# Doubled tail columns for the transposes, weights loaded by whole rows, and a newly searched TensorE order in a two-layer attention and feed-forward kernel

The kernel runs on **one core of one Trainium2 chip**. The metric is the device time of one execution in microseconds (us), as the median of some runs. The profile is one execution, and all profiled runs in this text were fast ones.

## The reference, cut to what matters

```python
def _A_ref(x, mem0, Wq, Wk, Wv, Wo, seg_len):        # x [1, 2048, 576], 32 heads of 128, bf16
    mem = mem0                                       # 8 rows
    for s in range(n_seg):                           # 64 segments of 32 tokens
        h = concat([mem, x[:, s*32:(s+1)*32]])       # 40 rows
        q, k, v = h @ Wq, h @ Wk, h @ Wv             # each 576 -> 32 x 128
        p = softmax(where(mask, q k^T * scale, -1e9))
        o = (p v) @ Wo
        mem = o[:, :8]                               # goes into the next segment
        outs.append(o[:, 8:])
    return concat(outs)
# _B_ref: silu(x @ w1) * (x @ w3) @ w2, 576 -> 4608 -> 576
x = x + _A_ref(_layernorm(x), ...);  x = x + _B_ref(_layernorm(x), ...)
x = x + _A_ref(_layernorm(x), ...);  x = x + _B_ref(_layernorm(x), ...)     # the same weights again
```

The memory makes the 64 segments of a layer a chain. The kernel fills the waits by running segment s of layer 0 beside segment s - 7 of layer 1, in 71 steps.

## The kernel before

Matrices have 576 = 4 x 128 + 64 rows. The fifth chunk has only 64 rows, and Q, K and V need it in both halves of the 128 partitions: half the tail matmuls read the upper rows of the array, half the lower ones. So a group of 128 normalized tokens (tile XN) is transposed on TensorE into one PSUM bank, and from there copied to the tile HT in pieces. The fifth transpose takes columns 448 to 576, of which only the last 64 are new:

```python
def ln_tr(self, xn, b):
    for c in range(5):
        c0 = min(c * P, D - P)                       # the last one overlaps: 448
        self.mm(self.lnps(b)[:, c, :], self.T.XN[:, xn.i, c0:c0 + P], self.T.ident[:], True, True, is_transpose=True)

def ht_write(self, li, g, j, b):                     # one segment j of the group's four
    for x0, co, m in X_AT[self.kind(t, li), role(t)]:     # one piece (layer 0) or two of 24 and 8 (layer 1)
        self.cp(n, H_[:, 0:4, co:co + m], ps[:, 0:4, x0:x0 + m])
        for r in (0, R64):                                # the tail, into both halves
            self.cp(n, H_[r:r + R64, 4, co:co + m], ps[R64:P, 4, x0:x0 + m])

def load_qk(self, u):                                # u = 0..7: 512 columns of Wq and of Wk
    for kind, wd in ((0, self.a.wq), (1, self.a.wk)):
        self.dma(self.T.W[:, 4*kind:4*kind+4, c0:c1], wd[0:4*P, c0:c1].rearrange("(c p) n -> p c n", p=P))
    ...                                              # and the tails, 64 rows x 512 columns each
# order of the pieces: four of Q and K, four of V, four of Q and K, four of Wo
```

The order of all TensorE blocks is fixed by three strings, FIRST + FOUR x 11 + LAST, one letter to a block. Q and q are the projection to Q and K and its tail, S the scores, T the transpose of the probabilities, P their product with V, O and o the output projection and its tail, V v X x the V projections, F f W the feed-forward, `a` and `b` the transposes of a normalized group of layer 0 and layer 1, `n` that for the feed-forward, `p` the transpose of a group of step outputs (tile YTS). A period below is one repeat of FOUR. A planner in the kernel walks this order with estimated durations, gives each copy to ScalarE (ACT) or VectorE (DVE), and picks buffers; so a changed string or a changed copy also changes who does which copy.

```python
FOUR = (
    "QQqqpQQqqVSSvQnQqqFTQqfPSVvTFQPqfOFWOTooSfPXxWFTFfPfOOWooQQqqWFQqfSFQqfQQqqVXxvSSWWTQPqQTFPqfOFfSoWWFTOfPFOTWofP"
    "WFOfooQQqqQFfqFWWQfqVVSSvvQQqqFTWQqPfSTWQFfqFSPfOWWFfoTOPoTWPOaOoobWQQqqpQQSqqQQqqVSSXxvQqTQqPXSTOPoxTOPonTOPoOo"
)
```

## Time and profile before

| | before |
|---|---|
| median time | 2843.19 us (3 runs, 2841.11 to 2845.37) |
| TensorE (PE) busy / VectorE / ScalarE | 97% / 73% / 40% |
| copies HT from a bank / XTB from a bank | 558 / 96 instructions |
| first stage, until the second step starts | 63.66 us |
| the eleven repeats of FOUR | 1820.1 us |

A view's line for a group of instructions reads: start, length, engine, line, operation, output<-input, shapes, count, and in brackets the idle time of that engine just before and what ended it. PE and PEld are TensorE's matmuls and weight loads. "issue" as a releaser means that the engine waited for nothing that the profile shows. The lines of before stand in the prediction.

### The profile page before, as it was taken

How to read it: one execution, taken by the hardware profiler on the slowest of the kernel's cores; microseconds unless marked ns; L12 is line 12 of the kernel's file. 1: busy time of each engine (PE TensorE's matmuls, PEld its weight loads, DVE VectorE, ACT ScalarE, POOL GpSimd, SP SyncE). 2: the span in 40 equal slices, each digit the busy share in tenths (PEclk: the TensorE clock that was granted, in tenths of full speed). 3: DMA queues.
4: the chain of work that ended last, by engine and by line, in shares of the span. 5: the costliest groups of instructions: out<-in, count | busy, mean ns of one | idle time of the engine just before them, and what ended most of it. 6: DMA issues, size and time to landing. Idle time of an engine off the chain costs nothing.

```text
span 2838.2 us, 136886 instructions
## 1 busy us (share of the span) xinstructions
PE 2741.1 (97%) x60909; PEld 2257.2 (80%) x60909; DVE 2069.6 (73%) x5743; ACT 1144.9 (40%) x3629; POOL 328.4 (12%) x399
## 2 busy tenths in 40 slices
PE   5999999999999999999999999999999999999998
PEld 3787878788887878888787888878788887878786
DVE  4677767777777677777767777776777777777775
ACT  1434443443434344343434434343443435343332
POOL 1111110110101011010101101010110101010110
PEclk8999999999999999999999999999999999999998
DMA  9072514234241433424243342414334242423468
GB/s 301 4 201 81 167 48 142 70 103 139 62 136 58 139 88 99 138 62 136 59 138 89 96 140 63 135 57 139 88 99 138 63 135 63 141 80 107 142 176 242
DMA packets 493425, 323.84 MB, mean 114 GB/s; under 512 B 26680, under 2 KB 488000, under 8 KB 492832
## 3 DMA queue, kind: packets, MB, share of 16 engines
q1 hardware_dynamic: 489808, 308.15, 37.4%
q8 instruction: 476, 7.80, 1.2%
q0 software_dynamic: 3024, 6.93, 0.8%
q14 instruction: 117, 0.96, 0.1%
HBM read 310.26 MB, written 2.36 MB: 110 GB/s over the span
## 4 chain that ended last, share of the span: by engine, by line
PE 92%; DVE 3%; ACT 2%; DMA 2%; issue 1%; SPq 0%; POOL 0%; DVEq 0%; ACTq 0%
PE bank L539 80%; PE YB L539 12%; ACT HT L542 1%; DVE HT L545 1%; DMA W<-in_A_Wk_dram 1%; SPq L548 0%; DMA WO<-in_A_Wo_dram 0%; DVE XN L545 0%; DVE XR L545 0%; ACT OT L542 0%; DVE HTT L545 0%; DVE PB L545 0%; DVE STAT L545 0%; DVE LNS L545 0%; DVE SME L545 0%
## 5 line engine op out<-in xcount | busy, mean ns | idle before, releaser
L539 PEld LDWEIGHTS <-W 128*128 128x128 bf16 (+1 forms) x29040 | 1228.7, 99 | 156.6 <-issue 57.4
L539 PE MATMUL bank<-HT,W 128*128 128x80 bf16 (+3 forms) x22720 | 821.3, 198 | 23.4 <-ACT HT L542 11.6
L539 PE MATMUL bank<-XTB,W 128*128 128x256 bf16 (+3 forms) x6320 | 659.3, 262 | 0.2 <-DVE HT L545 0.2
L893 POOL MEMSET PB<- 128x1024 bf16 x284 | 270.0, 951 | 2117.9 <-PE bank L539 1837.0
L542 ACT ACTIVATE QKT<-bank 128x64 bf16<-128x64 f32 (+1 forms) x1371 | 316.6, 317 | 353.1 <-PE bank L539 347.8
L539 PE MATMUL YB<-OT,WO 128*128 128x80 bf16 (+3 forms) x11360 | 434.9, 199 | 22.6 <-ACT HT L542 14.2
L539 PEld LDWEIGHTS <-WO 128*128 128x128 bf16 (+1 forms) x11400 | 390.7, 102 | 62.5 <-issue 45.8
L539 PE MATMUL bank<-WV,HT 128*32 128x512 bf16 (+1 forms) x6840 | 383.1, 384 | 7.8 <-DMA WV<-in_A_Wv_dram 7.7
L545 DVE CAST QKT<-bank 128x64 bf16<-128x64 f32 (+2 forms) x693 | 186.4, 316 | 189.5 <-PE bank L539 186.4
L539 PE MATMUL bank<-W2C,HTT 128*128 128x288 bf16 x2232 | 315.6, 289 | 0.0
L542 ACT ACTIVATE HTT<-bank 128x512 bf16<-128x512 f32 (+1 forms) x324 | 178.4, 552 | 292.5 <-PE bank L539 291.2
L545 DVE TENSOR_TENSOR PB<-SME,STAT 40x128 bf16<-40x128 f32 (+1 forms) x1004 | 283.6, 321 | 15.5 <-DVE STAT L545 0.5
L539 PEld LDWEIGHTS <-HT 128*32 128x32 bf16 (+1 forms) x6840 | 149.6, 95 | 173.3 <-issue 44.2
L545 DVE TENSOR_REDUCE STAT<-SME 104x8 f32<-104x320 f32 (+1 forms) x568 | 270.5, 476 | 17.2 <-ACT SME L542 11.7
L545 DVE SCALAR_TENSOR_TENSOR XR<-bank,XR 128x288 f32<-128x288 f32 x576 | 243.5, 449 | 29.2 <-PE bank L539 23.2
L539 PEld LDWEIGHTS <-HTT 128*128 128x128 bf16 x2304 | 211.8, 98 | 57.0 <-issue 4.1
L545 DVE SCALAR_TENSOR_TENSOR HTT<-HTT,bank 128x512 bf16<-128x512 bf16 (+1 forms) x324 | 201.1, 621 | 54.0 <-ACT HTT L542 51.9
L542 ACT ACTIVATE SME<-SME 104x320 f32<-104x320 f32 (+1 forms) x284 | 133.6, 471 | 234.5 <-DVE SME L545 233.2
L542 ACT ACTIVATE PTS<-bank 128x320 bf16<-128x320 f32 (+1 forms) x387 | 149.1, 415 | 189.0 <-PE bank L539 156.2
L545 DVE TENSOR_TENSOR HTT<-HTT,bank 128x512 bf16<-128x512 bf16 (+1 forms) x324 | 203.6, 628 | 23.9 <-PE bank L539 0.5
L542 ACT ACTIVATE V<-bank 128x512 bf16<-128x512 f32 x256 | 141.8, 596 | 179.8 <-PE bank L539 177.7
L545 DVE TENSOR_TENSOR SME<-bank,maskb 104x320 f32<-104x320 f32 (+1 forms) x284 | 134.1, 485 | 109.3 <-PE bank L539 87.3
(63 smaller groups left out, 1774.6 us busy)
## 6 DMA issues: line engine op xcount, KB each, us to landing
W<-in_B_w_dram SPq DMA_DIRECT2D x612, 256.0 KB, 3.6
W2C<-in_B_w_dram SPq DMA_DIRECT2D x306, 288.0 KB, 3.2
W<-in_B_w_dram SPq DMA_DIRECT2D x612, 32.0 KB, 3.1
W<-in_B_w_dram SPq DMA_DIRECT2D x10, 512.0 KB, 9.6
XR<-in_A_x_dram POOLq DMA_DIRECT2D x16, 288.0 KB, 3.6
WO<-in_A_Wo_dram SPq DMA_DIRECT2D x4, 1152.0 KB, 11.5
W<-in_A_Wq_dram SPq DMA_DIRECT2D x8, 512.0 KB, 7.3
W<-in_A_Wk_dram SPq DMA_DIRECT2D x8, 512.0 KB, 7.3
```

The costliest lines, as they stand in the source:

```text
L539: self.ch("PE", self.nc.tensor.matmul(out, lhsT=lhsT, rhs=rhs, start=start, stop=stop, skip_group_check=True, **k))
L542: self.ch("ACT", self.nc.scalar.activation(*a, **k))
L545: self.ch("DVE", getattr(self.nc.vector, fn_)(*a, **k))
L893: return lambda n: self.ch("POOL", self.nc.gpsimd.memset(self.T.PB[:, pb.i], 0.0))
```

## The change

The intent has three parts. **Copies**: XN gets 64 more columns, a copy of its last 64. The fifth transpose then delivers the tail in both halves of the partitions, so one copy moves all five chunks; two neighbouring segments go into one copy as well, and in the planner each copy of a group depends on the one before. **Load**: Wq, then Wk, then Wv, by whole rows of 8 KB, 128 rows to a transfer. **Order**: all three strings searched anew with this model. The work of TensorE stays. The planner's estimates changed too: no copy is counted under 0.19 us, a normalization as 0.12 to 0.18 us longer, a load at 380 GB/s in place of 340.

```diff
 def ln_norm(self, src, xn):
-    self.v("tensor_scalar", self.T.XN[:, xn.i, :], ...)
+    self.v("tensor_scalar", self.T.XN[:, xn.i, 0:D], ...)
+    self.v("tensor_copy", self.T.XN[:, xn.i, D:D + R64], self.T.XN[:, xn.i, D - R64:D])
 def ln_tr(self, xn, b):
-    c0 = min(c * P, D - P)
-    ... self.T.XN[:, xn.i, c0:c0 + P] ...
+    ... self.T.XN[:, xn.i, c * P:(c + 1) * P] ...
-def ht_write(self, li, g, j, b):
+def ht_write(self, li, g, js, b):                     # js: one segment, or two neighbours
-    for x0, co, m in X_AT[...]: (three copies: four chunks, tail, tail)
+    if k:   cp(56, 24, 0, 40, 24); cp(0, 152, 24, 8, 8)      # layer 1: two copies for two segments
+    else:   cp(X_AT[0, role(t)][0][1], 80, 0, 32, 32)        # layer 0: one copy
 def xtb_write(self, bi, b):
-    (three copies)
+    return lambda n: self.cp(n, self.T.XTB[:, :, bi * P:(bi + 1) * P], self.lnps(b))
 def ln_nodes(...):
-    node("AD", cost, wr(b), deps=[d] + more, ...)
+    node("AD", cost, wr(b), deps=[d] + more + out[-1:], ...)
-def load_qk(self, u): (512 columns of four chunks of Wq and Wk, and of the tails)
+def load_qk(self, kind):
+    for c in range(4):
+        self.dma(self.T.W[:, 4 * kind + c, :], wd[c * P:(c + 1) * P, :])
+    self.dma(self.T.W[kind * R64:(kind + 1) * R64, 8, :], wd[4 * P:D, :])
   (Wv the same way; FIRST and LAST all new)
 FOUR = (
+    "QQpqqQQqqVSSvnQQqqFTQqPfSVvQTFfqPOOSooTWFfPWFTOPfFOfooQQqqQQSqqVXxvWTQWFfqFQqPfSSWFWQfqXxFTWQqfPOTOooSWFfPFTOfPW"
+    "OooWFQfqQFfqWQFfqWQFfqVSSVvvQQqqWTWQPqSQTFfqFfPSWOWFTfoOPoTWPOOooabWQQqqpQQSqqQQqqVSSvXxTQqQqPTSXPxOToOPoTOPnOoo"
```

More of the change, by code (lines that the diff above doesn't have):

```diff
@@ L164, in actc @@
 def actc(*ns):
-    return sum(0.067 + n * 0.000833 for n in ns)
+    return sum(max(0.067 + n * 0.000833, 0.19) for n in ns)
 def dve(*ns):
-    return sum(0.065 + n / 960.0 for n in ns)
+    return sum(max(0.065 + n / 960.0, 0.19) for n in ns)
 def dveh(*ns):
-    return sum(0.065 + n / 1920.0 for n in ns)
+    return sum(max(0.065 + n / 1920.0, 0.19) for n in ns)
 def ew(*ns):
@@ L187 @@
 FIRST = (
-    "amQQVqqQSQvQqqTVSvqQQXqPSTPQxqTOoqSOoPOTPOooQQqqQSQqqQSVqvTQqPQqSQqTSPOOTooPaTOPOooQQqqQQSqqQSQqqVvQTQPqqSTVPSOO"
-    "TovXPoTxPOOooQQqqQQSqqQqSVQqTvSQqPQqTSPOToPOOTooPOoQQqqQSpQqqVVvvnQTFfqQqSFfPQOQqqSTFfPoSWXOTFPfoxTOoPWOoFQfqQqF"
-    "QQqSqfQFfqSVvTWQFqPfaFfTOSoPQQqqFSWTOFPfoTOPfoOWoVFvQqfFQfqWSVvQFfqFTQfqWPSQQqqQSFqfTQqPWFfSOTFfoPOWToPOoOboQQqq"
-    "QSqXxQQqqQSqTQSQqqVvXPSTOPoTxOoPTPOOooQQpqqQQSqqQQnqqVvSSQTFqfVvFPfQTOqPWFToSfFOfPXxOFTWofPFOoofQQqqQSXxqQWFfqVv"
-    "QQTqqSFPfSFQQqfqOFSofTWPFTOfPoFTOPfWOFooQqfFQqfQWQSqVqvQFqfSTWQqFPfSVvQTaQqqWFSFfPfOToPWTOoPObOXooxQQpqqQQSqQqqV"
@@ L193 @@
-    "QqSTSvQPQqqOTPSnXxTOoPoTOPOooVvpQQqqQqSQQqqnQSqVvTFfPQTOFPqfSQFqfXxOWTWoSoXxFfPFTOPfoWWOFfoFQqQfqQWQqqFWSSfVvQFf"
-    "qWQqFTQqfPSQWOTFqPfoSOWWTFfPoFTOPfWOooVvWQQqqFQfSqFWQqfQQSqqWTFfPQFSqQqfOTWWaFSPfVTOovWPTOoPobOoQQqqpQQSqqXVvxSQ"
-    "qQTqQqSQPqnTOPSXxoTOPoWTOPoOo"
+    "amQQqqQSqQqQSqQTQqqQSqSVvVvPXTPTOoOPoTOPoOoxQQqqQQSqqQSqVvQqQTSQPqqOTSoPTPOOToPaOooQQqqQQSqqQQSqVqvTQSqQPqVSTOPv"
+    "oTOoPXTOPOxooQQqqQSQqqQSqQqVSvQqTQqPTSOPToPOOTooPOoVvpQQqqQSQqqnVSvFfTQQqqQFPqfSFQfqXSTFfPOTOoWPxoTOFfPFOooWQqQq"
@@ new lines @@
+    "fFfSQQqqWQSQqqVvTFfPSFTfPQOQFfqqOTSWFooPfFTOPoaOoWfQQqqFQfqSVvWQFfqQqVSvWQqFfTQqFPfSTQqOWFofSPTFfPOWTOoPObooQQqq"
+    "XxSQQqqQQqqSTQVqvQqSPSTXxOPoTOPToPOOooQQqqpQQqqSVvnQQqqSTFfPFQqfSOTQqPFWOFffSVoTvXPxWOTFofPFOofoQQqqQqSQWQqqVvTQ"
+    "PSFfqQFqfSXxWTQFqPfOToSFafPOFofOTWPFOfooQFqfWQqVvSQqQFfqFQfqSQTWqQqPSFQqfVSvTWOPFFffoTOPoTWPOoOboQQqqQQSqqXVvxSQ"
+    "TpQqqXPxSQqTQqPOSoTOPoOTPnOooQQqqQpQSqQqqQnqVSvQTFfqFSPfVvQFfqTOFPfXxoSWWOTFfPXFTxofPOWOWooQQqqQqSQWFqfQQqqSTWFF"
+    "ffVvSQPqWTFQOqPfoSWTOFfPoFTOPfWOWooQFfqQqWFWQqfSVvFQqWfSFQqfQqWTQQPSqqVFTSvfPOWWoTFfOPoTWPOOooabQQqqpQQSqQqqVXxv"
@@ L196 @@
+    "STQQqqQPqSTOSoPXxOTWPTnoPOOoo"
 )
 FOUR = (
-    "QQqqpQQqqVSSvQnQqqFTQqfPSVvTFQPqfOFWOTooSfPXxWFTFfPfOOWooQQqqWFQqfSFQqfQQqqVXxvSSWWTQPqQTFPqfOFfSoWWFTOfPFOTWofP"
-    "WFOfooQQqqQFfqFWWQfqVVSSvvQQqqFTWQqPfSTWQFfqFSPfOWWFfoTOPoTWPOaOoobWQQqqpQQSqqQQqqVSSXxvQqTQqPXSTOPoxTOPonTOPoOo"
+    "QQpqqQQqqVSSvnQQqqFTQqPfSVvQTFfqPOOSooTWFfPWFTOPfFOfooQQqqQQSqqVXxvWTQWFfqFQqPfSSWFWQfqXxFTWQqfPOTOooSWFfPFTOfPW"
+    "OooWFQfqQFfqWQFfqWQFfqVSSVvvQQqqWTWQPqSQTFfqFfPSWOWFTfoOPoTWPOOooabWQQqqpQQSqqQQqqVSSvXxTQqQqPTSXPxOToOPoTOPnOoo"
@@ L200 @@
 )
 LAST = (
-    "QQpqQqqQSqnQQFqSqfVVSvvQTFPqfTOQqPWTOSoXxPoFTFfPfOOWQooFqfFQqWWQqfVXxvSWFQfqWFTSfQqQqPQFQSqqfOTFWPfSoWOTFoPfFWWT"
-    "OfPFOfooWQQqqFWQQqqSfVvQWFfqQSqTWQSqPFQfqVSvOWWTFfPFofTOPoTWPOoOobQQqqpQQSqqQQSqqVTSXxXvxQPqTQqPSWOToOoPTnPOOooQ"
-    "QqqQpQqqSVSvQqVvQnqTQPqSFfTQFqPfOoSOTFfPFTOofPXWOxooWQQqqVvFQfqWQSqWQFqfSFfTQqQWSqWFfPQFfqTOWWFPSofTOFfPWWOTFoof"
-    "PFOoWQqfQqWFQQqSqfFQfqVSvWQqTWQqSPQFqfFfSTWOWoFPfVvTWWPOoTOPbOooQqpQQqqXxSQnQqqQFfqSFfVvSTQPqFfTQqWSFOPfoFTOPfoT"
-    "OPWOFooQqfFQfqQQqqSVvQqSWTQqPQSVvqFTQPfqOOSooTFfPXxOTFPWOoofQQqqFfQQSqqWQQqqSFTfVFfvWSQqPQFfqOTSoFPfWTOoPFTOfPFO"
@@ L207 @@
-    "fooQQqqWQqVSVvvQqQQSTqQqQPqSqTOSPOoToPTPOOoopFfnWFfFFffFfWFWFffFfFWfFFffWFFffWFWfFfFFffWFfFfWW"
+    "QQqqVvpQQSqqQnQSqqQqTFPQfqVvSFOTFPfoSfTOPXxWFfOWTFofPFOooWWQfqQqFQfqSWQqXVvxSQWQqqFTfQFPfqSTOWWQPqFoSfFTOfPoWTOP"
+    "WOooFQqfQFfqQVSvqWQWFfqFSQfqQqWTWFSfPQQqqWFfSTWOFfPoVvTWPOoTOPobOoQQqqQQSqqQQpqqVSvSQqQTqXxSPTXxPOToOPoTWPOOoonQ"
+    "QqqpQqSVvQnQqqQSqTFfPVSvQQqqFTOPoSfOTFWWofPFTOfPXOWooQxqWQFqfVvSQQqFfqQQSqqQqTFfPSWWFQfqFfOWWFTSofPFTOWPfoTFPfOO"
+    "WooQQqqFQQqfqSWFWQFqffSVvWTWQQqqQqVSSvFPfFTOWWfFPfToOPoTWOPoOWboQQqqpQqSVXnvxQFfqQQqqTSSQPqFfQFfqWTSOPFTOofPFTof"
@@ L208 @@
+    "POOooWQFqfQFfqQQSqqVSvWQQqqTQPqSFQqfVTFfPvSOTOXooxPWTFPOOfooQQqqQFSqfVQFqfvWQTFSqQfqQFqPSfQqWTOPoSFfTOoPFWTOfPFO"
+    "fooQQqqQQSqqVvQWQSqqVvSQTQqPqTOPSoTFPOoOTofPOopnWFfFFfFffWFWfFfFfFfWFfWFfFFffWFfWFfFFffWFfFfWW"
 )
@@ L216, with make_nodes @@
     ustep, mode_pen, hor, wait, bulk, ff_split, last_win, tail_at = 0.0315, 0.1194, 0.0162, 0.141, 0.02, False, 2.5, -1.5
-def make_nodes(em, nseg, pools, o=Opt, dma_bw=230e3, load_bw=340e3):
+def make_nodes(em, nseg, pools, o=Opt, dma_bw=230e3, load_bw=380e3):
     ngrp = nseg // 4
@@ L246, in make_nodes @@
     ld_m0 = load("m0", kb(8, D), -10, em.load_m0())
-    ld_qk, ld_v, ld_o = {}, {}, {}
-    pr = -9.0
-    for what, i in [("qk", 0), ("qk", 1), ("qk", 2), ("qk", 3), ("v", 0), ("v", 1), ("v", 2), ("v", 3), ("qk", 4),
-                    ("qk", 5), ("qk", 6), ("qk", 7), ("o", 0), ("o", 1), ("o", 2), ("o", 3)]:
-        pr += 0.1
-        if what == "qk":
-            ld_qk[i] = load("ldqk", kb(1152, 512), pr, em.load_qk(i))
-        elif what == "v":
-            ld_v[i] = load("ldv", kb(576, 1024), pr, em.load_v(i))
-        else:
-            ld_o[i] = load("ldo", kb(1024, 576), pr, em.load_o(i))
+    ld_qk = [load("ldqk", kb(576, 4096), kd - 9.0, em.load_qk(kd)) for kd in (0, 1)]
+    ld_v = [load("ldv", kb(576, 4096), -7.0, em.load_v())]
+    ld_o = [load("ldo", kb(1024, 576), g - 6.0, em.load_o(g)) for g in range(NG)]
     b = banks(1)
@@ L273, in ln_nodes, with ht_set @@
         p_ = node("POOL", 0.45, em.ln_pow(xn), deps=[a], prio=prio, name=tag + "pow")
-        c = node("DVE", 0.34 if src is xn else 0.48, em.ln_norm(src, xn), deps=[p_], prio=prio, name=tag + "norm")
+        c = node("DVE", 0.46 if src is xn else 0.66, em.ln_norm(src, xn), deps=[p_], prio=prio, name=tag + "norm")
         b = Slot("bank", users=len(writes))
         d = node("PE", 5 * 0.056, em.ln_tr(xn, b), deps=[c], prio=prio, mode="full", acq=[b], rel=[xn], name=tag + "tr")
-        return [node("AD", cost, wr(b), deps=[d] + more, prio=prio, rel=[b], name=tag + "wr") for wr, cost, more in writes]
+        out = []
+        for wr, cost, more in writes:
+            out.append(node("AD", cost, wr(b), deps=[d] + more + out[-1:], prio=prio, rel=[b], name=tag + "wr"))
+        return out
     def ht_writes(li, g):
-        out = []
+        out, at = [], {}
+        for j in range(4):
+            at.setdefault((4 * g + j - role(4 * g + j + LAG * li)), []).append(j)
+        for te, js in at.items():
+            te += LAG * li - R_HT
+            cost = ewh(240, 80) if li and both(te + R_HT) else ewh(160 * len(js))
+            out.append(((lambda js: lambda b: em.ht_write(li, g, js, b))(js), cost, reads_ht.get(te, []) + reads_ht.get(te + 1, [])))
+        return out
+    def ht_set(li, g, nodes_):
+        i = -1
         for j in range(4):
             t = 4 * g + j + LAG * li
-            te = t - role(t) - R_HT
-            cost = ewh(96, 32, 24, 8, 24, 8) if li and both(t) else ewh(128, 32, 32)
-            out.append(((lambda j: lambda b: em.ht_write(li, g, j, b))(j), cost, reads_ht.get(te, []) + reads_ht.get(te + 1, [])))
-        return out
-    def ht_set(li, g, nodes_):
-        for j in range(4):
-            ht_ready[li, 4 * g + j + LAG * li] = nodes_[j]
+            i += j == 0 or role(t) == 0
+            ht_ready[li, t] = nodes_[i]
     vx_slots, vx_nodes, vx_pe, last_v = {}, {}, [None], [None]
@@ L327, in step @@
             sl, ev, last_v[0] = v_nodes("VM", t, pv_, o.vmt, (lambda k: lambda b, tail: em.vm(t, k, b, tail))(k), 2 if e else 4,
-                                     hm[:1] + hx + (list(ld_v.values()) if t == 0 else []), hm[1:])
+                                     hm[:1] + hx + (ld_v if t == 0 else []), hm[1:])
             for kk in ((k,) if e else (0, 1)):
@@ L342, in step @@
                 pq = t + o.qk + o.ustep * u
-                m_ = node("PE", 32 * mm80, em.qk(t, u, b), deps=hx + hm[:1] + ([ld_qk[u]] if t == 0 else []),
+                m_ = node("PE", 32 * mm80, em.qk(t, u, b), deps=hx + hm[:1] + (ld_qk if t == 0 else []),
                           prio=pq, mode="full", acq=[q] + b, name="QK")
@@ L423, in job @@
         prev_ff = last_up[0]
-        cost = ewh(512, 128, 128)
+        cost = ewh(640)
         for (bi, g) in reversed(ents):
@@ L588, in load_m0 @@
         return lambda n: self.dma(self.T.M0[0:MEM, :], self.a.mem0[0])
-    def load_qk(self, u):
+    def load_qk(self, kind):
         def f(n):
-            c0, c1 = u * 512, (u + 1) * 512
-            for kind, wd in ((0, self.a.wq), (1, self.a.wk)):
-                self.dma(self.T.W[:, 4 * kind:4 * kind + 4, c0:c1], wd[0:4 * P, c0:c1].rearrange("(c p) n -> p c n", p=P))
-            for kind, wd in ((0, self.a.wq), (1, self.a.wk)):
-                self.dma(self.T.W[kind * R64:(kind + 1) * R64, 8, c0:c1], wd[4 * P:D, c0:c1])
+            wd = (self.a.wq, self.a.wk)[kind]
+            for c in range(4):
+                self.dma(self.T.W[:, 4 * kind + c, :], wd[c * P:(c + 1) * P, :])
+            self.dma(self.T.W[kind * R64:(kind + 1) * R64, 8, :], wd[4 * P:D, :])
         return f
@@ L602, in wv, with load_v @@
         return self.T.WV[:, 0:4 * H * E].rearrange("p (c n) -> p c n", c=4)
-    def load_v(self, g):
+    def load_v(self):
         def f(n):
-            k, r = g // 2, g % 2
-            c0, c1 = g * 1024, (g + 1) * 1024
-            self.dma(self.wv(False)[:, :, c0:c1], self.a.wv[0:4 * P, c0:c1].rearrange("(c p) n -> p c n", p=P))
-            self.dma(self.wv(True)[r * R64:(r + 1) * R64, k * 1024:(k + 1) * 1024], self.a.wv[4 * P:D, c0:c1])
+            for c in range(4):
+                self.dma(self.wv(False)[:, c, :], self.a.wv[c * P:(c + 1) * P, :])
+            t = self.a.wv[4 * P:D, :].rearrange("p (k r n) -> p k r n", k=2, r=2)
+            for r in (0, 1):
+                self.dma(self.wv(True)[r * R64:(r + 1) * R64, :].rearrange("p (k n) -> p k n", k=2), t[:, :, r, :])
         return f
@@ L616, in load_xn @@
     def load_xn(self, g, xn):
-        return lambda n: self.dma(self.T.XN[:, xn.i, :], self.a.x[g * P:(g + 1) * P, :])
+        return lambda n: self.dma(self.T.XN[:, xn.i, 0:D], self.a.x[g * P:(g + 1) * P, :])
     def load_x(self, g, xr):
@@ L687, in src_ap @@
     def src_ap(self, src):
-        return self.T.XN[:, src.i, :] if src.pool == "xn" else self.T.XR[:, src.i, :]
+        return self.T.XN[:, src.i, 0:D] if src.pool == "xn" else self.T.XR[:, src.i, :]
     def ln_stats(self, src, xn):
@@ L708, in f @@
             L = self.T.LNS[:, xn.i]
-            self.v("tensor_scalar", self.T.XN[:, xn.i, :], self.src_ap(src), L[:, 12:13], L[:, 15:16],
+            self.v("tensor_scalar", self.T.XN[:, xn.i, 0:D], self.src_ap(src), L[:, 12:13], L[:, 15:16],
                    op0=ALU.subtract, op1=ALU.mult)
+            self.v("tensor_copy", self.T.XN[:, xn.i, D:D + R64], self.T.XN[:, xn.i, D - R64:D])
         return f
@@ L719, in f, with cp @@
             for c in range(5):
-                c0 = min(c * P, D - P)
-                self.mm(self.lnps(b)[:, c, :], self.T.XN[:, xn.i, c0:c0 + P], self.T.ident[:], True, True, is_transpose=True)
+                self.mm(self.lnps(b)[:, c, :], self.T.XN[:, xn.i, c * P:(c + 1) * P], self.T.ident[:], True, True, is_transpose=True)
         return f
-    def ht_write(self, li, g, j, b):
+    def ht_write(self, li, g, js, b):
         def f(n):
             ps = self.lnps(b)
-            t = 4 * g + j + LAG * li
-            H_ = self.ht(t)
-            for x0, co, m in X_AT[self.kind(t, li), role(t)]:
-                x0 += j * SEG
-                self.cp(n, H_[:, 0:4, co:co + m], ps[:, 0:4, x0:x0 + m])
-                for r in (0, R64):
-                    self.cp(n, H_[r:r + R64, 4, co:co + m], ps[R64:P, 4, x0:x0 + m])
+            t = 4 * g + js[0] + LAG * li
+            H_, x0, k = self.ht(t), js[0] * SEG, self.kind(t, li)
+            def cp(co, gap, src, apart, m):
+                d, r = H_[:, :, co:co + m], ps[:, :, x0 + src:x0 + src + m]
+                if len(js) == 2:
+                    d, r = (bass.AP(v.tensor, v.offset, [list(x) for x in v.ap][:-1] + [[by, 2], [1, m]]) for v, by in ((d, gap), (r, apart)))
+                self.cp(n, d, r)
+            if k:
+                assert len(js) == 2
+                cp(56, 24, 0, 40, 24)
+                cp(0, 152, 24, 8, 8)
+            else:
+                cp(X_AT[0, role(t)][0][1], 80, 0, 32, 32)
         return f
     def xtb_write(self, bi, b):
-        def f(n):
-            ps = self.lnps(b)
-            dst = self.T.XTB[:, :, bi * P:(bi + 1) * P]
-            self.cp(n, dst[:, 0:4, :], ps[:, 0:4, :])
-            for r in (0, R64):
-                self.cp(n, dst[r:r + R64, 4, :], ps[R64:P, 4, :])
-        return f
+        return lambda n: self.cp(n, self.T.XTB[:, :, bi * P:(bi + 1) * P], self.lnps(b))
     def v_mm(self, t, b, strips, tail):
@@ L1076, in fin_cast @@
     def fin_cast(self, xr, xn):
-        return lambda n: self.act(self.T.XN[:, xn.i, :], self.T.XR[:, xr.i, :], ACT.Copy)
+        return lambda n: self.act(self.T.XN[:, xn.i, 0:D], self.T.XR[:, xr.i, :], ACT.Copy)
     def store(self, g, xn, last):
-        return lambda n: (self.dma if last else self.swdma)(self.a.out[g * P:(g + 1) * P, :], self.T.XN[:, xn.i, :])
+        return lambda n: (self.dma if last else self.swdma)(self.a.out[g * P:(g + 1) * P, :], self.T.XN[:, xn.i, 0:D])
 class Tiles:
@@ L1137 @@
     T.XTB = sp.tile([P, 5, 2 * P], BF, name="XTB")
-    T.XN = sp.tile([P, pools["xn"], D], BF, name="XN")
+    T.XN = sp.tile([P, pools["xn"], D + R64], BF, name="XN")
     T.LNS = sp.tile([P, pools["xn"], 16], F32, name="LNS")
```

## The prediction

> **What bounds the kernel now.** I read the page first, then the table by stages, then TensorE's waits and the instruction timeline around them.
>
> ```profile
> span 2838.2 us, 136886 instructions
> ...
> PE 2741.1 (97%) x60909; PEld 2257.2 (80%) x60909; DVE 2069.6 (73%) x5743; ACT 1144.9 (40%) x3629; POOL 328.4 (12%) x399
> ...
> PE bank L539 80%; PE YB L539 12%; ACT HT L542 1%; DVE HT L545 1%; DMA W<-in_A_Wk_dram 1%; SPq L548 0%; DMA WO<-in_A_Wo_dram 0%; DVE XN L545 0%; DVE XR L545 0%; ACT OT L542 0%; DVE HTT L545 0%; DVE PB L545 0%; DVE STAT L545 0%; DVE LNS L545 0%; DVE SME L545 0%
> ```
>
> TensorE is busy 97% of the span and is 92% of the chain that ended last. The change keeps all 60,909 matmuls, so only TensorE's idle time (97.1 us = 2838.2 - 2741.1), its slow-clock time and its changes of array shape can move. The table by stages (first column the stretch, then length, busy us by engine, granted clock, DMA share, GB/s) says where the idle time is:
>
> ```profile
> 0.00:63.66 63.66, 30.70 (x706) 21.69 (x707) 26.65 (x69) 10.76 (x34) 10.99 (x27) 0.89 1.05 324
> 63.66:532.60 468.94, 454.97 (x11278) 376.03 (x11277) 341.51 (x983) 194.04 (x645) 59.99 (x69) 0.99 0.38 109
> 532.60:2356.00 1823.40, 1792.29 (x38490) 1479.61 (x38486) 1355.03 (x3751) 762.05 (x2394) 204.52 (x243) 1.00 0.36 103
> 2356.00:2801.20 445.20, 430.38 (x9999) 353.25 (x9998) 324.27 (x886) 169.21 (x534) 52.32 (x60) 0.98 0.44 128
> ```
>
> 33.0 us are idle before the second step starts at 63.66 us, with the DMA share over 1: the first step waits for weights. Another 14.0, 31.1 and 14.8 us lie in the three later stages. The third is eleven equal periods of 165.8 us (four steps each, the string FOUR). One period's waits, in the timeline (start, length, engine, instruction, count, idle before it and who ended it; cut to the place that matters):
>
> ```profile
> 1195.86 0.69 ACT L542 ACTIVATE HT<-bank 128x128 bf16<-128x128 bf16 x3 [0.77 <-PE bank L539]
> 1196.58 0.61 DVE L545 COPY HT<-bank 128x128 bf16<-128x128 bf16 x3 [1.02 <-ACT HT L542]
> 1197.22 0.69 ACT L542 ACTIVATE HT<-bank 128x128 bf16<-128x128 bf16 x3 [0.67 <-DVE HT L545]
> 1197.93 0.22 ACT L542 ACTIVATE HT<-YB 128x64 bf16<-128x64 f32 x1
> 1197.94 0.61 DVE L545 COPY HT<-bank 128x128 bf16<-128x128 bf16 x3 [0.75 <-ACT HT L542]
> 1198.20 0.34 PE L539 MATMUL YB<-OT,WO 128*64 128x80 bf16 x8 [0.97 <-ACT HT L542]
> ...
> 1198.58 0.58 DVE L545 TENSOR_SCALAR XN<-XR,LNS 128x576 bf16<-128x576 f32 x1
> ...
> 1199.22 0.45 PE L539 MATMUL bank<-ident,XN 128*128 128x128 bf16 x5 [0.68 <-DVE XN L545]
> ```
>
> One transposed group is copied to HT by twelve instructions that ACT and DVE run strictly in turn, 1195.86 to 1198.55: 2.69 us. The copy of the new memory (HT<-YB) queues behind them on ACT, the normalization (XN) behind them on DVE, and TensorE waits 0.97 + 0.68 us. In every second period the throttle then halves the clock for one interval:
>
> ```profile
> 1199.80:1203.20 3.40, 3.40 (x38) 2.87 (x37) 2.07 (x12) 1.51 (x8) 0.00 (x0) 0.50 0.33 95
> 1203.20:1206.60 3.40, 3.40 (x98) 3.27 (x96) 2.93 (x11) 2.74 (x11) 0.59 (x1) 1.00 0.24 84
> ```
>
> [...] (1) [...] The trace shows the half clock for 3.4 us at 1199.8, but after a stretch only partly idle (2.36 of 4.00 us busy just before)[...]. (2) [...] on DVE 128x128 into HT takes 224 ns, 128x32 174; on ACT 278 and 197. A quarter of the elements costs over 70% of the time. (3) [...] 326 GB/s while Wq and Wk come in pieces of 512 and 64 KB, 379 while Wo comes in pieces of 1152 KB:
>
> ```profile
> DMA packets 5602, 6.20 MB, mean 326 GB/s; under 512 B 288, under 2 KB 4860, under 8 KB 5602
> ...
> DMA packets 4076, 4.55 MB, mean 379 GB/s; under 512 B 72, under 2 KB 4073, under 8 KB 4073
> ```
>
> (the DMA view of 3 to 22 us and of 48 to 60 us).
>
> **The change part by part.**
>
> *Loading.* Wq, Wk and Wv are 3 x 4.72 = 14.16 MB. At 326 to 330 GB/s they take 43.2 us; in DMAs of 1 MB at Wo's 379 they would take 37.4. Sixteen transfers (with the tails of 64 rows) replace forty. I take that as 5.8 us sooner: Wq complete at about 16 us, Wk 28, Wv 41, the last Wo piece at 55 to 56 instead of the 61.5 where the chain now leaves it ("DMA WO" 49.34 + 12.16). The price: no projection can start before Wk is complete, where now it starts at 15.1 us. So TensorE has the whole first step after 28 us. From rows of the timeline: eight Q and K blocks of 32 matmuls near 0.9 us plus tails, scores, transposes and slow clock, some 13 us, end near 41 as Wv arrives. After that come two V blocks at 2.3 (4.6), one further V block (2.4), four output blocks with tails at 1.3 (5.2), three transposes and four PV blocks (2.8), changes of shape and evacuation waits (2 to 3): 17 to 18 us. So the second step starts at 58 to 60 against 63.66. Gain 4 to 6 us; I take **5**.
>
> *Copies.* A first-layer group goes from 12 instructions to 3 (160, 320, 160 elements), a second-layer one from 24 to 4 (240 and 80 twice), XTB from 3 to 1. By the slopes of (2), 0.84 ns per element on ACT and 0.52 on DVE: 305 + 440 + 241 = 0.99 us in place of 2.69, and (372 + 237) + (282 + 199) = 1.09 in place of the 4.80 from 1199.70 to 1204.50. XTB 640 elements: 0.70 on ACT for 1.14, 0.49 on DVE for 0.88. Against it one copy of 64 columns per normalization, near 0.16 us x 64 = 10 us of DVE, each on the way to the transpose. Busy time falls from 141 us (HT 59.0 + 49.1, XTB 22.7 + 10.5) to about 63 with the new copies. DVE at 73% and ACT at 40% bound nothing, so almost none of these 78 us is gain in itself; what counts is TensorE's wait.
>
> *Order.* In the built kernel the period's end reads O, O, tails, then the first-layer transpose, then the second-layer one. On ACT the memory copy now stands ahead of the HT copies, and on DVE so does the normalization. From the starts of matmuls (they count pipelined time better than the idle column): that tail started 1.16 us late, and elsewhere, where no HT copy is in the way, the same wait is 0.51, so 0.65 is gained; the second-layer transpose's lateness of 0.77 goes; the half clock costs about 1.6 us (38 matmuls where 98 fit, but many of them 288 wide), in every second period, so 0.8. Against it: the strings' changes between ways of using the array (full, half rows, strips of columns) go from 109 to 112 per period and from 2,115 to 2,150 in all; one costs 95 ns (an 80-column matmul is followed after 36 ns by its like and after some 131 by another shape), so 0.28 per period, 3.3 us in all. Net 0.65 + 0.77 + 0.8 - 0.28 = 1.94 per period, x 11 = **21 us**.
>
> In the stage before, the same chain stands at 84.96 (1.18 idle), 222 to 228, 368.81 (1.70) and a half-clock interval at 370: about **6 us**. In the stage after, TensorE waits 1.8 us for HT at 2679 and the clock halves at 2681: **3 us**.
>
> Sum: 2843.2 - 5 - 21 - 6 - 3 = **2808 us**, 1.2% less.
>
> **Rivals.** *The gap is only filled otherwise*: the new order has other tight places, and the 64-column copy and the chained copies lengthen the way from XN to the next step. The old order too was searched, and lost 3 us per period to what its search had not seen. Against it: the chained copies are what the hardware did anyway (each group waits for the one before), so this search sees them. It would leave loading and a little: 2830 to 2840. *The load does not speed up*: rows of 1 KB and of Wv's 2 KB run alike (326 and 330 GB/s), so longer rows may give nothing; then the late start of TensorE costs and the first step ends at 63 to 66: 2813 to 2816. *The search closes nearly all gaps*: waits of 0.44 and 0.34 in the period, and a 0.7 wait for YTS in every second one, would go too, with more in the stages before and after: 50 to 60 us in all, 2785 to 2793. For over 2% the kernel must fall below 2786, that is recover 57 of 97 idle us, and part of those is the load, which cannot vanish.
>
> **Range and chances.** The load is sure to 4 us, the period to 1 us (11 us in all), the two other stages to 5. Added in one direction this is 20 us: 2787 to 2829. Faster by over 2%: 0.10; within 2%: 0.89; slower: 0.01.
>
> **What would show it.** In the changed profile: GB/s of the first 50 us near 375, not 325; the second step's first matmul at 58 to 60 us; HT from bank in about 109 instructions and XTB in 32; a chain of about 1.0 and 1.1 us in place of 2.69 and 4.80; a period of 163 to 164.5 us; no half-clock interval in most periods. A period still at 165.8 with a wait on another tile, or GB/s unchanged, would prove me wrong.

"The slopes of (2)" come from the four measured copies there: (278 - 197) / 96 = 0.84 ns per element on ACT, (224 - 174) / 96 = 0.52 on DVE. The 0.16 us for an added copy was an estimate; the nearest copy in the trace of before, HT<-mem0T with 128x40, took 164 ns.

## The result

The changed kernel took **2800.55 us** (median of 4 fast runs, 2798.39 to 2805.53), the kernel before 2844.28 us beside it. The ratio is **0.985** (95% interval 0.9832 to 0.9867), 1.5% less: within 2%, and inside the range of 2787 to 2829, 7.5 us under the predicted 2808. A ratio here is the mean time of one kernel's fast runs over that of the other's fast runs of the same rounds, so not quite the ratio of the medians. The results of all kernels were correct. The medians of the kernel before beside the experiments were 2846.88 (e1 to e4), 2846.20 (e5, e6, e8, e9) and 2844.97 us (e7, e10).

The page of the changed kernel:

```profile
span 2798.6 us, 136339 instructions
...
PE 2730.5 (98%) x60909; PEld 2252.9 (81%) x60909; DVE 2018.1 (72%) x5501; ACT 1116.7 (40%) x3422; POOL 328.4 (12%) x399
```

The span fell by 39.6 us. Busy time of PE fell by only 10.6 us with the same matmuls (20.5 us at half clock in place of 61.4), its idle time from 97.1 to 68.1. The table by stages (the stretch, its length, busy us by engine, granted clock, DMA share, GB/s) is cut at the block starts that answer to one another in the two kernels:

```profile
0.00:59.50 59.50, 28.66 (x706) 21.06 (x707) 23.56 (x60) 10.69 (x33) 10.82 (x27) 0.91 1.00 349
59.50:553.04 493.54, 484.09 (x12134) 399.64 (x12126) 360.31 (x1022) 203.64 (x656) 65.60 (x76) 1.00 0.37 104
553.04:2352.13 1799.09, 1787.14 (x38438) 1479.01 (x38435) 1319.49 (x3586) 742.54 (x2244) 204.00 (x242) 1.00 0.36 104
```

To cut exactly I counted matmuls in the trace: the strings say how many each block has, so the start of every block is known. A block is called late below by what its start exceeds the usual gap for its kind (the fifth percentile of such gaps in the same trace, and 95 ns where the shape of the array changes: after an 80-column matmul the next of its shape starts at some 36 ns, one of another shape at some 131). Before and after compare as follows, and the last two columns come from runs told further down.

| stage (us) | before | after | change | predicted | copies only | new order and load only |
|---|---|---|---|---|---|---|
| until the second step | 63.66 | 59.50 | -4.2 | -5 | 62.74 | 61.11 |
| to the first repeat of FOUR | 506.1 | 493.5 | -12.6 | -6 | 496.2 | 505.2 |
| eleven repeats | 1820.1 | 1799.1 | -21.0 | -21 | 1788.9 | 1832.5 |
| the rest | 448.3 | 446.5 | -1.9 | -3 | 448.8 | 451.2 |

The "predicted" sum of 35 is short of 39.6 mainly by one stage, the second. What the table does not tell is which part of the change earned it. The place at the end of a period where TensorE had waited 0.97 and 0.68 us looks so in the timeline after:

```profile
1175.11 0.58 DVE L544 TENSOR_SCALAR XN<-XR,LNS 128x576 bf16<-128x576 f32 x1 [0.67 <-POOL LNS L702]
1175.73 0.18 DVE L544 COPY XN<-XN 128x64 bf16<-128x64 bf16 x1
1175.89 0.22 ACT L541 ACTIVATE HT<-YB 128x64 bf16<-128x64 f32 x1 [1.91 <-PE YB L538]
1176.16 0.33 PE L538 MATMUL YB<-OT,WO 128*64 128x80 bf16 x8 [0.32 <-ACT HT L541]
...
1176.43 0.73 PE L538 MATMUL bank<-ident,XN 128*128 128x128 bf16 x10
...
1176.92 0.63 ACT L541 ACTIVATE HT<-bank 128x160 bf16<-128x160 bf16 x2 [0.15 <-PE bank L538]
...
1177.20 0.63 DVE L544 COPY HT<-bank 128x240 bf16<-128x240 bf16 x3
...
1177.75 0.54 ACT L541 ACTIVATE HT<-bank 128x240 bf16<-128x240 bf16 x2
```

Both groups' ten transposes now run back to back at 1176.43 (x10), the normalization and its 0.18 us copy are done before, and the memory copy on ACT is not behind anything but TensorE. HT is filled from banks in 109 instructions (67 on ACT, 42 on DVE) and XTB in 32, as predicted. All seven copies of both groups here take from 1176.92 to 1178.29, 1.37 us, where the two chains of before took 2.69 and 4.80. No interval at half clock is left in the eleven periods; before had four of 3.4 us, not one in every second period as predicted.

The first stage's chain of work, in order of time (start, length, what), for the changed kernel:

```profile
2.01 6.94 DMA W<-in_A_Wq_dram
...
8.97 20.39 DMA W<-in_A_Wk_dram
...
33.94 1.77 issue
...
39.76 2.70 issue
```

The first seven projection matmuls follow the pieces of Wq and Wk one by one as they land; the rest begins at 26.86, with Wk's last 128 rows, and its tail lands at 29.4. From there on TensorE waits for no weight in this stage, where before it still waited for Wo at 61.55 (0.83 us). Two waits for nothing that the profile shows follow.

### The profile page after: what moved, and what is told of

It is laid out like the page before. It is cut to its first block, busy times and chain, and to the rows that moved or that the text cites. A ratio compares the mean times of both kernels' runs of the same rounds, so it can differ in the third digit from the quotient of the medians.

```text
span 2798.6 us, 136339 instructions
## 1 busy us (share of the span) xinstructions
PE 2730.5 (98%) x60909; PEld 2252.9 (81%) x60909; DVE 2018.1 (72%) x5501; ACT 1116.7 (40%) x3422; POOL 328.4 (12%) x399
## 3 DMA queue, kind: packets, MB, share of 16 engines
HBM read 310.26 MB, written 2.36 MB: 112 GB/s over the span
## 4 chain that ended last, share of the span: by engine, by line
PE 96%; DMA 1%; ACT 1%; issue 1%; DVE 1%; POOL 0%; SPq 0%; DVEq 0%; ACTq 0%; POOLq 0%
PE bank L538 83%; PE YB L538 14%; DMA W<-in_A_Wk_dram 1%; ACT HT L541 0%; DMA W<-in_A_Wq_dram 0%; ACT OT L541 0%; DVE STAT L544 0%; DVE SME L544 0%; DVE PB L544 0%; ACT PTS L541 0%; DVE HTT L544 0%; ACT SME L541 0%; DVE PTS L544 0%; DVE XR L544 0%; DVE XN L544 0%
## 5 line engine op out<-in xcount | busy, mean ns | idle before, releaser
L544 DVE TENSOR_TENSOR PB<-SME,STAT 40x128 bf16<-40x128 f32 (+1 forms) x1004 | 283.5, 321 | 15.5
L541 ACT ACTIVATE PTS<-bank 128x320 bf16<-128x320 f32 (+1 forms) x413 | 157.1, 414 | 177.6 <-PE bank L538 120.9
L541 ACT ACTIVATE OT<-bank 128x320 bf16<-128x320 f32 (+1 forms) x379 | 147.0, 412 | 171.1 <-PE bank L538 170.9
## 6 DMA issues: line engine op xcount, KB each, us to landing
W<-in_A_Wk_dram SPq DMA_DIRECT2D x4, 1024.0 KB, 16.8
```

Source lines behind the costliest of these rows:

```text
L541: self.ch("ACT", self.nc.scalar.activation(*a, **k))
L544: self.ch("DVE", getattr(self.nc.vector, fn_)(*a, **k))
```

## The experiments

### e1: the old pieces in the new sequence

```diff
 # changed kernel, but Wq and Wk in 8 x 512 columns, then Wv in 4 x 1024 columns
-    ld_qk = [load("ldqk", kb(576, 4096), kd - 9.0, em.load_qk(kd)) for kd in (0, 1)]
+    ld_qk = [load("ldqk", kb(1152, 512), 0.1 * u - 9.0, em.load_qk(u)) for u in range(8)]
```

> The changed kernel, but Wq, Wk, Wv come in the old pieces (512 KB in 1 KB rows, 1 MB in 2 KB rows, 64 and 128 KB tails), in the new sequence: all of Wq and Wk, then Wv, then Wo. Theory (larger transfers of longer rows speed the load up): the pieces landed every 3.64 us per Wq+Wk set and 3.5 per Wv set before, so Wk is complete near 32 us, Wv near 46 us instead of 43.4, Wo's last piece near 61; the second step starts near 62 us instead of 59.5, total 2802 to 2804 us. Rival (only the sequence counts): second step at 59.5, total within 1 us of the changed kernel's 2800.5.

Measured: 2805.03 us, ratio 0.9857 (0.9842 to 0.9872). From 3 to 44 us the DMA moved 323 GB/s, against 326 in the kernel before and 363 in the changed one. The ratio is not told apart from the changed kernel's. The second step began at 64.06 us, 4.6 us later than in the changed kernel and 1.9 later than in the slowest of the kernels with the same loads and first string (59.50 to 62.15, see below). The eleven periods took as long as there (1799.05 us), the stage before them 0.6 less and the last one 1.9 more. So with the old pieces the second step starts no earlier than before (63.66): the sequence alone gives none of the first stage's gain, and the larger transfers carry it. This rests on one profile of e1. (363 is below the 375 that I expected, for a reason that e5 shows.)

### e2: only the copies

```diff
 # kernel before with the doubled columns, the merged copies and the chain in the planner;
 # loads and all three strings of the kernel before
```

> The kernel before with its own loads and its own three order strings, but with the new transposes and copies (doubled 64 columns, one or two copies where there were three to six, chained). Theory (the length of the copy chain is the cause): the repeated period falls from 165.5 us to 163.3 to 164, no half-clock intervals in it, total 2812 to 2819 us. Rival (the new order is what gains): the period stays within 0.4 us of 165.5, total 2836 to 2843.

Measured: 2798.02 us, ratio 0.9831 (0.9815 to 0.9847). That is **the whole gain of the change** (0.985, and if anything more), without the new order and without the new loads; I had expected 2812 to 2819. The period is 162.60 us, 2.86 under before and 0.95 under the changed kernel. At the place shown above the three first-layer copies still stand ahead of the memory copy, but they now end before it is needed, and TensorE's wait is 0.32 us in place of 0.97:

```profile
1177.02 0.83 ACT L549 ACTIVATE HT<-bank 128x160 bf16<-128x160 bf16 x3 [0.77 <-PE bank L546]
...
1178.43 0.22 ACT L549 ACTIVATE HT<-YB 128x64 bf16<-128x64 f32 x1 [0.59 <-PE YB L546]
1178.71 0.33 PE L546 MATMUL YB<-OT,WO 128*64 128x80 bf16 x8 [0.32 <-ACT HT L549]
```

My account of the order as the part that frees the waits is wrong.

### e3: only the new order and the new loads

```diff
 # changed kernel's strings and loads; copies, columns and planner of the kernel before
```

> The kernel before with the new loads and the new order strings, but the old transposes and copies (12 and 24 copies per group). Theory (chain length): the waits come back at another place, behind the second-layer transpose; period 165 to 167 us, total 2818 to 2836. Rival (the order alone gains, by letting the memory copy go ahead of the HT copies): period 163.5 to 164, total 2801 to 2806.

Measured: 2851.85 us, ratio 1.0023 (1.0008 to 1.0038): no gain, and slower than even the theory's 2818 to 2836. The period is 166.59 us, 1.13 over before and within the theory's 165 to 167. Together with e2 this makes a square of four, all in us per period:

| | order before | order changed |
|---|---|---|
| copies before | 165.46 | 166.59 |
| copies changed | 162.60 | 163.55 |

The copies take off 2.86 or 3.04, whichever the order; the new order of FOUR puts on 1.13 or 0.95, whichever the copies. The two effects nearly add, so neither enables the other. TensorE's waits in one period say what stands behind it (engine, line, what was waited for: us in total, times, longest). First before, in a period without half clock, without the two waits that the prediction shows; then e3:

```profile
PE bank L539 <- DVE YTS L545: 0.6, 1, 0.6
PE bank L539 <- ACT HT L542: 0.3, 1, 0.3
PE YB L539 <- ACT OT L542: 0.2, 1, 0.2
```

```profile
PE bank L531 <- DVE HT L537: 1.6, 1, 1.6
PE YB L531 <- ACT HT L534: 0.9, 3, 0.3
PE bank L531 <- DVE XR L537: 0.8, 1, 0.8
```

With the new order and old copies the wait does not go; it moves to the first Q of the next step (1.6 us for HT) and to XR, which queues behind the copies on DVE.

### e4: one letter moved

```diff
 # kernel before; the first-layer transpose a moved beside b, as in the changed order
-    ...TWPOaOoobWQQqqp...
+    ...TWPOOooabWQQqqp...
```

> The kernel before, with one letter of the repeated string moved: the first-layer transpose stands behind the last output block and its tails, as in the new string, and nothing else is changed. If the place of that transpose is the cause: the late tail falls from 1.16 to 0.5 us and the second-layer transpose's wait goes, period 163.9 to 164.3, total 2826 to 2832. If the length of the chain is: the period falls by less than 0.7 us or not at all, total 2836 to 2846, with a wait for HT before the next Q block.

Measured: 2849.8 us, ratio 1.0012 (0.9997 to 1.0027), above both stated totals; period 165.63 (165.72 in the mean of the eleven), so no gain, as for the chain's length. The waits at the memory copy (late by 0.51, not 1.16) and at `b` shrink as in the changed kernel, and what they free is lost at the next Q (late by 1.73) and at the transpose p (0.90). This is what the new string did in e3, in one letter. Taking the copies out of the way of one wait by order put them in the way of another; only making them short removes both.

### e5: the tails first, on two queues

```diff
 # changed kernel; the 64-row tails of Wq, Wk and Wv issued first, alternately by SyncE and ScalarE
+    def load_tails(self):
+        for kind, wd in ((0, self.a.wq), (1, self.a.wk)):
+            (self.adma if kind else self.dma)(self.T.W[kind*R64:(kind+1)*R64, 8, :], wd[4*P:D, :])
+        ... the same for the two halves of Wv's tail
```

> The changed kernel, with the four 64-row tails of Wq, Wk and Wv moved to the very start and issued in pairs from two engines (SP for partitions 0 to 63, ACT for 64 to 127), then the 1 MB transfers in the same sequence. In the changed kernel a 512 KB tail took as long as a 1 MB transfer of 128 rows (2.47 against 2.49 us). Theory (a transfer into half of the partitions runs at half the rate, two such into different halves at once run at the full rate): tails done by 6.5 us, Wk by 27, Wv by 37 to 38 instead of 43.4, Wo by 50; the second step starts at 55 to 56.5 instead of 59.5; total 2796 to 2798. Rival (TensorE's own work after Wk, or its instruction fetches, set the first step): second step at 58.5 to 60, total 2800 to 2802.

Measured: 2800.45 us, ratio 0.9842 (0.9826 to 0.9859); the expected gain was missed. The reason to try was a pair of lines of the changed kernel's DMA view, the whole-chunk transfers from 4.0 to 13.4 us and Wq's tail from 13.6 to 16.7. The third line is the same view of e5, from 3 to 10.2 us:

```profile
DMA packets 546, 3.99 MB, mean 424 GB/s; under 512 B 59, under 2 KB 59, under 8 KB 59
...
DMA packets 110, 0.77 MB, mean 248 GB/s; under 512 B 16, under 2 KB 16, under 8 KB 16
```

```profile
DMA packets 464, 1.58 MB, mean 220 GB/s; under 512 B 72, under 2 KB 80, under 8 KB 336
```

A tail of 0.52 MB into 64 partitions took 2.47 us, as long as 1.05 MB into 128 (one landed every 2.49 us), and its 8 KB packets took 620 ns in the middle (495 to 680) against 309. So this transfer into 64 partitions ran at half the rate; what holds it there, the runs do not show. That two queues would fill both halves of the partitions at once, at the full rate, was a guess of mine, and it failed: both queues were at work (65.7% and 37.8% of the 16 engines' time in that stretch), yet the total stayed at 220 GB/s, and the landings of Wk's, Wv's first, Wq's and Wv's second tail began one after another, at 5.12, 6.40, 8.82 and 10.06. So here a second queue brought nothing. The three tails cost 7.2 us in place of some 3.7 at the full rate (1.57 MB over 424 GB/s, an estimate from the lines above), which is why loading was slower than predicted.

The load is only half of the answer, though. In e5 Wk was complete at 30.5 (29.4 in the changed kernel), Wv at 41.9 (43.4) and Wo at 54.8 (56.9), and still the second step began at 61.41, not at 55 to 56.5. So the rival has the cause right, though not its 58.5 to 60: in this step the end does not wait for Wv or Wo. What holds TensorE up after Wk stands under "What stays open".

### e6: the same bytes with runs of 2 KB

```diff
 # changed kernel; each 1 MB transfer as 1024 columns of all four chunks
-    for c in range(4): self.dma(self.T.W[:, 4*kind + c, :], wd[c*P:(c+1)*P, :])
+    for c0 in range(0, H*E, 1024):
+        self.dma(self.T.W[:, 4*kind:4*kind+4, c0:c0+1024], wd[0:4*P, c0:c0+1024].rearrange("(c p) n -> p c n", p=P))
```

> The changed kernel, but the 1 MB transfers of Wq, Wk and Wv take 1024 columns of four row blocks (2 KB runs) instead of whole 8 KB rows; number and size of the transfers and the tails are the same. Theory (the length of the run sets the rate): 2.95 us per transfer as Wv had before, instead of 2.49, so Wv is complete near 49 instead of 43.4, second step at 64 to 65, total 2804 to 2806; and TensorE's two waits of 1.77 and 2.70 us with no cause shown, which stand beside its instruction fetches, shrink below 1 us each. Rival (the size of the transfer alone counts): Wv complete within 1 us of 43.4, total within 1.5 us of 2800.5.

Measured: 2802.65 us, ratio 0.9848 (0.9833 to 0.9863), not told apart from the changed kernel. A transfer landed every 2.71 us, 9% slower than with rows of 8 KB, and Wv was complete at 46.47 in place of 43.44. So size and row length each give a part: 323 GB/s from 3 to 44 us in e1, 345 here, 363 in the changed kernel. The two "issue" waits were still there (0.74 and 3.21 us, together 3.95 against 4.47), so long rows are not their cause.

### e7: no chain in the planner

```diff
 # changed kernel
-    deps=[d] + more + out[-1:]
+    deps=[d] + more
```

> The changed kernel, but the planner no longer makes each copy of a transposed group depend on the one before; everything else as changed. Theory (the engines take the copies of one group one after the other anyway, since each copy is found waiting for the one before; the chain in the planner only tells it what happens): the period stays within 0.2 us of 163.55 and the time within 5 us of the changed kernel's 2800.6. Rival (a planner that believes in parallel copies spreads them badly over the two vector engines): the period grows by over 0.5 us, the time by over 6 us.

Measured: 2805.3 us, ratio 0.9862 (0.9846 to 0.9879), period 163.74 against 163.55. Both of the theory's bounds just hold. The 0.19 us is one late Q after W, in every period, so the chain in the model is worth some 2 us of 1799; the rest of the 4.8 us lies mainly in the first step (61.03 against 59.50) and the end (447.7 against 446.5), which vary between kernels that differ in nothing there.

### e8 and e9: the old FOUR in the changed kernel

```diff
 # e8: changed kernel with FOUR of the kernel before.  e9: e5's loads as well.
```

> The changed kernel, with the repeated string FOUR of the kernel before; first and last strings, loads and copies new. The copies-only run had a period of 162.60 us with the old string, the changed kernel 163.55 with the new one. If that difference belongs to the string itself: period 162.60, total 2800.5 - 11 x 0.95 = 2790 us (2788 to 2792). If it belongs to how the three strings fit together: period 163 or more, or a loss at the seams, total 2795 or more.

> The two-queue tails and the old repeated string together. If the two gains add: 2790 - 3 to 4 = 2785 to 2788 us, over 2% faster than the kernel before (2843 to 2847 here). If the load gain is not real, 2790 as the run with the old string alone.

Measured: e8 **2791.99 us**, ratio 0.9815 (0.98 to 0.9829); e9 2792.45 us, ratio 0.9811 (0.9796 to 0.9825), the two not told apart. Both beat the kernel before, and both intervals end just below that of the changed kernel (0.9832 to 0.9867). e8's prediction holds; e9's 2785 to 2788 was missed, as the two-queue loads added nothing. Neither is shown to be over 2% faster, and e8 is not told apart from e2 (0.9815 to 0.9847). The period of e8 is 162.60 us, that of e2 to the hundredth. TensorE's waits in one period, first the changed kernel, then e8:

```profile
PE YB L538 <- ACT HT L541: 0.9, 3, 0.3
```

```profile
PE bank L538 <- ACT HT L541: 0.7, 2, 0.3
PE YB L538 <- ACT HT L541: 0.3, 1, 0.3
PE YB L538 <- ACT OT L541: 0.3, 1, 0.3
```

The idle time is even larger in e8, 1.3 against 0.9 us, so the idle column does not hold the 0.95 us, and block starts, which count pipelined time, must say it. In the changed order three output tails start 0.51 late and one output block 0.31; in e8 it is one tail 0.51, then 0.44 and 0.35. That is 1.84 against 1.30, 0.54 us more. Three more changes of the array's shape, at 95 ns, make 0.28. The last 0.13 is spread over lateness of under 0.05 each.

### e10: no pairs

```diff
 # changed kernel with the doubled columns, but a copy for each segment
-    cost = ewh(240, 80) if li and both(te + R_HT) else ewh(160 * len(js))    # 3 and 4 copies for a group
+    cost = ewh(120, 40) if li and both(te + R_HT) else ewh(160 * len(js))    # 4 and 8 copies
```

> The changed kernel with the doubled columns, but one copy for each segment, not one for two neighbouring segments: four copies of 160 elements per partition for a first-layer group in place of three, eight (120 and 40) for a second-layer group in place of four. Theory (what counts is that the 64-row tail no longer needs copies of its own): a chain of 1.1 and 1.8 us in place of 1.0 and 1.1, the period 163.6 to 164.1, the time 2801 to 2807. Rival (the pairs matter as much, every copy counts by its fixed cost in the wait): the period 164.5 or more, the time 2812 or more.

Measured: 2800.5 us, ratio 0.985 (0.9833 to 0.9867), period 163.55 like the changed kernel's. Twelve copies take from 1176.42 to 1178.26 here, 1.84 us in place of 1.37, and it costs nothing measurable. Of the merging, then, the doubled columns (three copies into one) gave the gain; the pairs came after the wait had already gone. (Tried with the new order only.)

## Why the prediction was right, and where it was wrong

**Loading: right in direction, and its size is uncertain: 4.2 us of 5 in these two profiles.** Wq, Wk and Wv were complete at 16.8, 29.4 and 43.4 (predicted 16, 28, 41), Wo at 56.9 (55 to 56), the second step at 59.5 (58 to 60). Rival two, that longer rows change nothing, fell with e1. What I did not price are the half-rate tails, some 3.5 us. From Wk to the first V block at 43.96 it took 14.6 us, not 13, of which 4.5 were the two waits of 1.77 and 2.70 that I had not foreseen; from there to the second step 15.5, not 17 to 18. The term itself is only sure to 3 us: kernels with the very same loads and first string started the second step at 59.5, 59.75, 61.03, 61.11 and 62.15 (after, e10, e7, e3, e8), those with the old loads and first string at 63.66, 62.74 and 64.35 (before, e2, e4). The means, 60.7 and 63.6, differ by 2.9 us.

**The periods: the sum of 21 was right, its split was not.** The pieces that I listed held: the memory copy late by 0.51 and not 1.16, `b` no longer late, the half clock worth about 1.6 in the periods that had it (a Q late by 0.66 and one by 0.96), three changes of shape. But I gave them to the new order, and e2 shows that the copies alone bring them about. (The half clock does not speak for the copies: four intervals of 3.4 us came in the eleven periods of before, the first after a stretch with TensorE busy 2.36 of 4.00 us, and none in those of the changed kernel; but none came in those of e3 and e4 either, which keep the old copies and have longer waits, one Q 1.7 us late and the next `p` 0.9. So the runs do not show what halves the clock.) Two things were missed, of opposite sign. In the periods without half clock, blocks at the same place were late by 0.12, 0.70, 0.18 and 0.12 us, behind the second-layer copies (the 0.6 for YTS in the lines under e3 is of this), and these waits go too. I had seen a wait of 0.7 and placed it in rival three. So the place is worth (4 x 1.62 + 7 x 1.12) / 11 = 1.30 us per period, not 0.8: the half clock adds only 0.5 to a wait that is always there. With 0.2 inside the period's last P block that makes 0.65 + 0.77 + 1.30 + 0.2 = 2.92, and the copies measure 2.86, where my terms for them sum to 0.65 + 0.77 + 0.8 = 2.22. Against that the new FOUR costs 0.95, where I had 0.28. The failed step is "Net 0.65 + 0.77 + 0.8 - 0.28 = 1.94": its result met the measured 1.91 because the errors of +0.64 and +0.67 cancel. Rival one, that the new order has other tight places, was true of the order; rival three, that the 0.7 goes as well, was true of the copies.

**The stage before: 6 predicted, 12.6 measured.** This is where most of the 7.5 us of the total come from (the rest lies between runs: the medians differ by 43.7 us, the two profiled runs by 39.6). I cut that stage at 532.6 and listed its waits, then took the repeats as eleven equal periods; what lies between 532.6 and the first repeat at 569.8 was in neither list. There stood the longest wait of the whole middle of the run. Before:

```profile
534.46 1.22 ACT L542 ACTIVATE HT<-bank 128x96 bf16<-128x96 bf16 x6 [0.92 <-PE bank L539]
535.72 2.26 DVE L545 COPY HT<-bank 128x96 bf16<-128x96 bf16 x12 [1.41 <-ACT HT L542]
...
538.01 1.22 ACT L542 ACTIVATE HT<-bank 128x96 bf16<-128x96 bf16 x6 [2.33 <-DVE HT L545]
539.26 0.22 ACT L542 ACTIVATE HT<-YB 128x64 bf16<-128x64 f32 x1
...
539.53 1.67 PE L539 MATMUL bank<-HT,W 128*128 128x80 bf16 x42 [3.70 <-ACT HT L542]
```

and the same place in e2, with the order unchanged:

```profile
526.97 0.89 ACT L549 ACTIVATE HT<-bank 128x240 bf16<-128x240 bf16 x4 [0.70 <-PE bank L546]
...
528.68 1.49 PE L546 MATMUL bank<-HT,W 128*128 128x80 bf16 x37 [0.34 <-ACT HT L549]
```

Twenty-four copies of a second-layer group, 4.77 us in turn, hold the memory copy and with it the next step by 3.70 us; four copies hold it by 0.34. This wait and the 6 us of the list make 9.4, and the copies alone measure 9.9 in this stage. The other 2.7 come with the new FIRST: with the changed copies the stage takes 496.2 with the old string and 492.3 to 493.8 with the new one. So unlike FOUR, the new FIRST is an improvement, of 2.4 to 3.9 us against one profile of e2 (the loads differ too, but the stage starts after the second step). With the old copies it was worth 0.9 (e3: 505.2 for 506.1).

**The last stage: 3 predicted, 1.9 measured.** The waits for HT that I named at 2679 and the half clock at 2681 are gone. The stage is the noisiest: kernels that differ only in loads or in the copies' pairing took 444.9 to 448.4 us, so I do not split 1.9 us further. At 2760.23 TensorE still waits for XN at the end of the last step, 3.38 us where before had 1.94, on the chain of reduce, normalize and the added copy (0.18). That does not make this piece worse: before had twenty feed-forward matmuls of 2.24 us standing in the same stretch, and from the transpose of YTS to that of XN it took 4.69 us before and 4.09 after.

**The price of the 64 extra columns**, which I had put at 0.16 us each, is 181 ns, 64 times, and none of it was found on the end of a wait in the periods.

**What stays open** is the pair of "issue" waits of 1.77 and 2.70 us in the first step. Each followed a 16,384 B packet of the queue that the page calls instruction (q8), which took 1.02 and 1.33 us beside the weight load (DMA share 1.06 and 1.05 meanwhile), and TensorE began again 1.45 to 1.48 us after the packet's end in four of four cases (two in the changed kernel, two in e8). The other traces add to this. In all eight kernels with the new first string and transfers of 1 MB (after, e3, e5 to e10) the second stop stands before the same matmul, the 352nd; TensorE goes on 1.41 to 1.56 us after such a packet's end, and the second step starts 16.9 to 17.7 us after that. So the second step's start (59.5 to 62.2) follows the moment at which this packet ended (41.0 to 43.4). There are 476 such packets in a run, one for every 256 of TensorE's 121,818 matmuls and weight loads. That TensorE waits for its instructions is therefore likely, but not shown: nothing in the kernel issues those transfers, and no run moved them on purpose.

## What to carry to other kernels

When one change repairs a data path and brings a newly searched schedule with it, measure the square of four: here the repair alone gave the whole gain and the new repeated part of the schedule took some 9 us of it back (e8 against the changed kernel), which the comparison of the two kernels alone did not tell. When many small copies stand in one queue, ask first which of them exist only because of the layout of their source: 64 duplicated columns, written once, removed two of every three copies and the waits of TensorE behind them, while merging further gave nothing. When adding up waits from a trace, cut the stages where the schedule's parts begin and end, or the largest one may fall between two lists.
